# Scatters of a routing table without an order between them, and a prologue spread over two queues: a fused attention and two-layer mixture-of-experts kernel

## The chip, the cores and the metric

The kernel runs on one core of a Trainium2 chip. The core has TensorE for matrix products (PE in the rows, its weight loads PEld), VectorE (DVE), ScalarE (ACT), GpSimd (POOL), and SyncE (SP), which here only issues transfers. ScalarE and GpSimd issue transfers too; each engine works through its own list in order, so a transfer that has to wait for something holds up all that stands behind it on that engine. The metric is the device time of one execution in microseconds (us).

## The reference, cut to what matters

Three layers follow each other. First comes attention with a decay: 2 batches, 8 heads, 768 positions, 64 numbers per head, in blocks with a running state.

```python
Dmask = np.where(rel >= 0, lam[:, None, None] ** rel[None, :, :], 0.0)
lam_pow = lam[:, None, None] ** (pos[None, :, None] + 1)
...
intra = np.einsum('bhic,bhjc->bhij', qb, kb) * Dmask[None]
intra = np.einsum('bhij,bhjd->bhid', intra, vb)
inter = np.einsum('bhid,bhde->bhie', qb * lam_pow[None], kv_state)
out[:, :, sl] = intra + inter
kv_state = lam_block[None, :, None, None] * kv_state + np.einsum('bhsd,bhse->bhde', kb_dec, vb)
```

Its output, 1536 rows of 512 numbers, goes through two mixture-of-experts layers with 8 experts each. A row goes to the one expert with the largest logit, and is weighted with that expert's probability:

```python
expert_idx = np.argmax(logits, axis=1)
...
for e in range(E):
    mask = expert_idx == e
    h = np.maximum(x[mask] @ w1[e], 0.0)
    out[mask] = gate_w[mask, None] * (h @ w2[e])
```

So the rows have to be sorted by expert between the layers. The kernel does that through tables in device memory (HBM).

## The kernel before, in words

**Attention** runs over 12 tiles of 128 rows, one per stage `s` of a loop; the two batches alternate. Stage `s` computes the scores of tile `s` (`st_A`, L420), lets GpSimd scale its operands (`st_pool`: `qd` L433, `kd` L437, `ds` L444), multiplies the scores by the decay mask `Dm` on VectorE (L425), turns the finished tile `s-2` into rows and stores it to the table of rows `xd` (`st_rows`, L496 to L503), and finishes tile `s-1` (`st_B`: L456 with `qd`, L461 with the masked scores; `st_S` L475 for the state). The output needs `qd` of a tile one stage after GpSimd is to make it. `load_X` (L141) loads tile `s+3`, 1 MB, at the end of a stage, into four buffers. From stage 5 on SyncE also loads one 512 KB block of weights of the first expert per stage (`raw`, L354), and from stage 6 on ScalarE copies one block per stage (`whi`, L361) ahead of the next stage's own copies.

**Routing of the first layer** is done beside it. `st_pick` finds a row's expert, `st_rank` its place in that expert's list (`posk`), and after every three tiles `Gates` computes the probabilities into `rec1`. Then `scat` (L550) sends the three tiles' records to `tab1` in HBM: an indirect transfer per tile, issued by GpSimd, 128 records of 8 bytes, to places that `posk` gives. The program's dependency tracking sees twelve writes to one table and lets each wait until the one before has landed. They are issued in stages 5, 8 and 11, three at a time, and the last three, of the tiles `LATE`, after the loop. The first expert's list is read from the table at the end of stage 11 (`tb0`, L615), without the tiles in `LATE`, which are brought in by matrix products (L584). Rows are then gathered (L636), transposed (L655), and the first expert starts (L825). The next expert's list (`tb`, L747) is read after all twelve scatters; its rows are gathered at L768 and transposed at L788.

**The second table** `tab2` has its own sixteen scatters (L960). Those go through `put`, which declares that they don't depend on each other and lets GpSimd write one number after each (`gap`, L281); `after_puts` lets a reader of the table wait for all of them.

**The prologue** makes the powers of `lam` by eight short steps on VectorE (L191, L194), which double the number of powers each time, sends them to HBM (`F_d`, L196), and reads them back in two shapes: the decay mask `Dm` (L201, two halves of 256 KB, made of 512-byte pieces) and `qtab` (L207). All of these are in SyncE's list, between the first loads of `X`; `emb`, `tau` and `wgs` are sent from ScalarE's (L145 to L147).

A completed transfer is seen through one of eight semaphores that SyncE's and ScalarE's transfers take in turn, so the ninth transfer waits until the first has landed, and so on. The `init_dram` transfers (L225 to L232) clear the tables after stage 1.

Of the kernel before, what the change touches and what calls it, by code (L numbers as in the profile page):

```python
# [15 lines left out]
AF = mybir.ActivationFunctionType  # L16
ALU = mybir.AluOpType
# [58 lines left out]
def body(ctx, tc, nc, A, O):  # L76
# [5 lines left out]
    tab1 = dram.tile([E * TS, 2], I32, name="tab1")  # L82
# [108 lines left out]
    nc.vector.tensor_copy(out=F_s[:, 128:129], in_=lam)  # L191
    for s in range(7):
        n = 1 << s
        nc.vector.tensor_scalar(out=F_s[:, 128 + n:128 + 2 * n], in0=F_s[:, 128:128 + n],  # L194
                                scalar1=F_s[:, 127 + n:128 + n], scalar2=None, op0=ALU.mult)
    nc.sync.dma_start(out=F_d, in_=F_s)  # L196
    load_X(1, 0)
    f0 = F_d[0:8, :]
    Dm = ac.tile([128, 8, 128], F32, name="Dm")
    for g in range(2):  # L200
        nc.sync.dma_start(  # L201
            out=Dm[:, 4 * g:4 * g + 4, :],
            in_=bass.AP(tensor=f0.tensor, offset=f0.offset + 256 * g, ap=[[1, 128], [512, 4], [1, 128]]))
    load_X(1, 1)
    qtab = ac.tile([128, 4, 128], F32, name="qtab")
    for hh in range(2):
        nc.sync.dma_start(out=qtab[64 * hh:64 * hh + 64],  # L207
                          in_=bass.AP(tensor=f0.tensor, offset=f0.offset + 256 * hh + 128,
                                      ap=[[0, 64], [512, 4], [1, 128]]))
    load_X(2, 0)  # L210
    load_X(2, 1)
    load_X(3, 0)
    load_X(3, 1)
# [59 lines left out]
    puts = []  # L273
    gap = const.tile([1, 1], F32, name="gap")

    def put(inst):

        for p in puts:
            tc.declare_no_dep(inst.ins, p.ins, reason="distinct rows")
        puts.append(inst)  # L280
        nc.gpsimd.memset(gap, 0.0)  # L281

    def after_puts(inst):
        for p in puts:
            tc.add_manual_dep(inst.ins, p.ins.name, mybir.DependencyInfo(mybir.DependencyClass.Sync, mybir.DependencyReason.DATA), reason="rows of the table")
# [441 lines left out]
    class Expert:  # L727
# [601 lines left out]
```

## Time and profile before

| | us |
|---|---|
| median of 3 runs | 499.51 (494.91 to 502.37) |
| the profiled execution's own time | 493.88 |
| its span, first to last instruction | 492.1 |
| TensorE busy | 433.0 (88%) |
| VectorE busy | 336.9 (68%) |
| ScalarE busy | 269.7 (55%) |
| GpSimd busy | 226.1 (46%) |

The mean granted clock of TensorE was 0.961 of full speed. Busy shares are averages over the attention loop (about the first 94 us) and two layers of experts; they say little about the loop. The views below are read for single stretches instead. In the timeline a row is: start in us, duration in us, engine, line, operation, output and inputs, and in brackets how long the engine had been idle before and what ended that; `SPq`, `ACTq` and `POOLq` are an engine's issuing side. Several equal instructions are merged into one row with a count.

### The profile page before, as it was taken

What the parts mean: (1) busy time and instruction counts of PE and PEld (TensorE: products, weight loads), DVE (VectorE), ACT (ScalarE), POOL (GpSimd) and SP (SyncE); (2) the same over time, 40 slices, a digit from 0 to 9 for tenths busy, and PEclk for the clock granted to TensorE, in tenths of its full rate; (3) what the DMA queues carried; (4) which work ended last, traced back from release to release, by engine and by line L of the source; (5) the groups of instructions that cost most, each with busy time, mean ns of one, the idle gap of its engine ahead of it and who ended that gap; (6) DMA issues with size and microseconds to landing.
All of it is one profiled execution on the core that took longest, in us unless ns stands there. A gap on an engine that the chain in (4) does not pass through costs nothing. (4 is left out here: it accounts for less than half of the span.)

```text
span 492.1 us, 9560 instructions
## 1 busy us (share of the span) xinstructions
PE 433.0 (88%) x3482; PEld 375.2 (76%) x3484; DVE 336.9 (68%) x714; ACT 269.7 (55%) x443; POOL 226.1 (46%) x224
## 2 busy tenths in 40 slices
PE   7696577759699999999999898999999999999980
PEld 3585566549578898988888797878987788988970
DVE  5454282525569888989888966853858588989950
ACT  2244253404467575665767445645768585776830
POOL 4641725415262738375574634403435725545520
PEclk9999697978899999999999999999999999999996
DMA  6998283231958485867658246483767767786400
GB/s 199 338 345 291 96 291 75 52 125 10 356 173 281 159 283 168 286 188 264 221 190 277 85 170 206 139 259 129 260 213 247 268 206 250 245 265 244 152 25 15
DMA packets 36693, 99.00 MB, mean 201 GB/s; under 512 B 10524, under 2 KB 12068, under 8 KB 35617
## 3 DMA queue, kind: packets, MB, share of 16 engines
q1 hardware_dynamic: 31569, 88.02, 53.7%
q0 software_dynamic: 4768, 10.28, 6.7%
q8 instruction: 29, 0.48, 0.4%
q14 instruction: 23, 0.19, 0.1%
q10 hardware_dynamic: 304, 0.03, 0.0%
HBM read 87.65 MB, written 11.21 MB: 201 GB/s over the span
## 5 line engine op out<-in xcount | busy, mean ns | idle before, releaser
L379 DVE SCALAR_TENSOR_TENSOR wlo<-raw,whi 128x1024 f16<-128x1024 f32 x98 | 128.8, 1316 | 33.0 <-ACT whi L361 32.1
L361 ACT ACTIVATE whi<-raw 128x1024 fp32r<-128x1024 f32 x128 | 131.3, 1050 | 5.2 <-DMA raw<-in_wa_dram 5.2
L373 POOL TENSOR_TENSOR wlr<-raw,whi 128x1024 fp32r<-128x1024 f32 x30 | 73.7, 2457 | 112.3 <-ACT whi L361 90.1
L795 PE MATMUL pm<-xT,whi 128*128 128x416 f32 (+8 forms) x416 | 99.2, 364 | 6.7 <-DVE xT L577 3.2
L795 PE MATMUL pm<-ht,whi 128*128 128x416 f32 (+7 forms) x384 | 86.7, 362 | 0.0
L795 PEld LDWEIGHTS pm<-xT,whi 128*128 128x128 f32 x416 | 68.8, 189 | 12.4 <-DVE xT L577 5.1
L795 PEld LDWEIGHTS pm<-ht,whi 128*128 128x128 f32 x384 | 66.8, 191 | 2.0
L801 PEld LDWEIGHTS <-wlo 128*128 128x128 f16 x720 | 57.2, 98 | 14.0 <-issue 8.6
L801 PE MATMUL pm<-xH,wlo 128*128 128x208 f16 (+11 forms) x512 | 59.4, 259 | 0.6 <-DVE xH L580 0.6
L845 ACT ACTIVATE ht<-t 128x416 fp32r<-128x416 f32 (+11 forms) x64 | 35.9, 561 | 27.4 <-DVE t L839 27.1
L851 DVE SCALAR_TENSOR_TENSOR ht<-t,ht 128x416 fp32r<-128x416 f32 (+11 forms) x64 | 42.6, 666 | 7.9 <-ACT ht L845 7.9
L838 ACT ACTIVATE t<-pm 128x416 f32<-128x416 f32 (+8 forms) x52 | 26.3, 506 | 33.9 <-PE pm L795 33.7
L839 DVE SCALAR_TENSOR_TENSOR t<-pm,t 128x416 f32<-128x416 f32 (+8 forms) x52 | 29.7, 571 | 14.8 <-ACT t L838 14.1
L960 POOL DMA_INDIRECT tab<-rec,pi x16 | 27.8, 1739 | 21.1 <-issue 7.3
L550 POOL DMA_INDIRECT tab<-rec,posk x12 | 11.9, 995 | 46.9 <-DMA tab<-rec,posk 25.4
L801 PE MATMUL pm<-ht,wlr 128*128 128x208 f32 (+8 forms) x208 | 33.4, 282 | 0.0
L967 POOL DMA_INDIRECT out_y_dram<-yr,tb x17 | 19.3, 1137 | 30.0 <-ACT yr L928 21.5
L574 ACT ACTIVATE xT<-pt 128x384 fp32r<-128x384 f32 (+9 forms) x33 | 16.8, 513 | 23.8 <-PE pt L788 11.9
L801 PEld LDWEIGHTS pm<-ht,wlr 128*128 128x128 f32 x208 | 29.1, 190 | 0.4
L768 POOL DMA_INDIRECT xr<-y2d,tb x17 | 24.1, 1416 | 9.3 <-issue 7.5
L801 PE MATMUL pm<-hh,wlo 128*128 128x208 f16 (+8 forms) x208 | 26.2, 256 | 0.0
L768 POOL DMA_INDIRECT xr<-xd,tb x14 | 23.4, 1670 | 4.4 <-issue 3.1
(197 smaller groups left out, 715.5 us busy)
## 6 DMA issues: line engine op xcount, KB each, us to landing
raw<-in_wa_dram SPq DMA_DIRECT2D x64, 512.0 KB, 5.5
raw<-in_wb_dram SPq DMA_DIRECT2D x64, 512.0 KB, 4.1
X<-in_att_dram SPq DMA_DIRECT2D x8, 1024.0 KB, 7.7
X<-in_att_dram SPq DMA_DIRECT2D x8, 512.0 KB, 6.1
xd<-xr SPq DMA_DIRECT2D x12, 256.0 KB, 4.6
y2d<-yr SPq DMA_DIRECT2D x2, 416.0 KB
y2d<-yr SPq DMA_DIRECT2D x2, 384.0 KB, 3.3
Dm<-F_d SPq DMA_DIRECT2D x2, 256.0 KB
```

Of the source, the lines that this page charges most:

```text
L361: nc.scalar.activation(out=f, in_=self.raw[g], func=AF.Copy, scale=self.scale(g))
L373: (nc.gpsimd if self.pat[g] == "p" else nc.vector).tensor_tensor(out=t.rearrange("p a b -> p (a b)"), in0=self.raw[g], in1=self.hi[g].rear ...
L379: nc.vector.scalar_tensor_tensor(out=t.rearrange("p a b -> p (a b)"), in0=self.raw[g], scalar=SW, in1=self.hi[g].rearrange("p a b -> p (a ...
L768: nc.gpsimd.indirect_dma_start(out=xr[0:n], out_offset=None, in_=self.rows, in_offset=bass.IndirectOffsetOnAxis(ap=idx[:, j, 0:1], axis=0))
L795: nc.tensor.matmul(pm[:, j, 0:2 * W].rearrange("p (a w) -> p a w", a=2), wh, s2, start=first, stop=last)
L801: nc.tensor.matmul(pm[:, j, 0:self.W], wl, sh, start=False, stop=False)
L838: nc.scalar.activation(out=t1, in_=pm[:, :, W:2 * W], func=AF.Copy, scale=sc)
L839: nc.vector.scalar_tensor_tensor(out=t2, in0=pm[:, :, 0:W], scalar=sc, in1=t1, op0=ALU.mult, op1=ALU.add)
L845: nc.scalar.activation(out=ht[:, :, 0, :], in_=t2, func=AF.Relu)
L851: nc.vector.scalar_tensor_tensor(out=ht[:, :, 1, :], in0=t2, scalar=0.0, in1=ht[:, :, 0, :].bitcast(F32), op0=ALU.max, op1=ALU.subtract)
L960: i = nc.gpsimd.indirect_dma_start(out=tab2[:, :], out_offset=bass.IndirectOffsetOnAxis(ap=self.pi[:, j:j + 1], axis=0), in_=rec2[0:n, rb[ ...
L967: i = nc.gpsimd.indirect_dma_start(out=O["y"], out_offset=bass.IndirectOffsetOnAxis(ap=self.tb[:, j, 1:2], axis=0), in_=self.yr[0:n, j, :] ...
```

## The change: what it does

Three things are changed.

- `scat` goes through `put` with a list of its own, `puts1`: the scatters of `tab1` no longer depend on each other, and GpSimd writes the `gap` number after each. The readers of the table (`tb0`, `tb`) wait for all the scatters recorded so far.
- The three scatters that were issued at the end of stage 5 are issued one per stage, in stages 6, 7 and 8 behind that stage's `st_pool`; those of stage 8 in stages 9, 10 and 11. Those of stage 11 and of `LATE` stay where they were.
- `lam`'s powers are made by ScalarE; `F_d`, `Dm` and `qtab` are sent from ScalarE's queue. SyncE issues the four halves of `X` for tiles 0 and 1 first, then `emb`, `tau`, `wgs`, then tiles 2 and 3.

```diff
     load_X(0, 0)
     load_X(0, 1)
-    nc.scalar.dma_start(out=emb, in_=A["emb"])
...
+    load_X(1, 0)
+    load_X(1, 1)
+    nc.sync.dma_start(out=emb, in_=A["emb"])
+    nc.sync.dma_start(out=tau, in_=A["tau"].to_broadcast([128, 1]))
+    nc.sync.dma_start(out=wgs, in_=A["wg"])
+    for i in (2, 3):
+        load_X(i, 0)
+        load_X(i, 1)
...
-    nc.vector.tensor_copy(out=F_s[:, 128:129], in_=lam)
...
-    nc.sync.dma_start(out=F_d, in_=F_s)
+    nc.scalar.activation(out=F_s[:, 128:129], in_=lam, func=AF.Copy)
+    for k in range(7):
+        n = 1 << k
+        nc.scalar.activation(out=F_s[:, 128 + n:128 + 2 * n], in_=F_s[:, 128:128 + n], func=AF.Copy,
+                             scale=F_s[:, 127 + n:128 + n])
+    nc.scalar.dma_start(out=F_d, in_=F_s)
...
-    def put(inst):
+    def put(inst, to=puts):
 
-        for p in puts:
+        for p in to:
             tc.declare_no_dep(inst.ins, p.ins, reason="distinct rows")
-        puts.append(inst)
+        to.append(inst)
         nc.gpsimd.memset(gap, 0.0)
...
     def scat(it):
-        nc.gpsimd.indirect_dma_start(out=tab1[:, :], out_offset=bass.IndirectOffsetOnAxis(ap=posk[:, it:it + 1], axis=0),
-                                     in_=rec1[:, it, :], in_offset=None)
+        put(nc.gpsimd.indirect_dma_start(
+            out=tab1[:, :], out_offset=bass.IndirectOffsetOnAxis(ap=posk[:, it:it + 1], axis=0),
+            in_=rec1[:, it, :], in_offset=None), puts1)
...
-    gates = None
+    gates, ready = None, []
     for s in range(12):
         ps = psf[s] if s < 2 else st_A(s)
         st_pool(s)
+        if ready:
+            scat(ready.pop(0))
...
         if gates:
             gates.gate()
-            for it in range(s - 5, s - 2):
-                scat(it)
+            ready += range(s - 5, s - 2)
             gates = None
+            while s == 11 and ready:
+                scat(ready.pop(0))
```

On **GpSimd**, in the loop from stage 5 to stage 8 (`tab_62` is `tab1`, `rec_69` is `rec1`), before:

```order
L433 TENSOR_TENSOR qd<-X,qtab 128x512
L437 TENSOR_TENSOR kd<-X,Dm 128x2x4x64
L444 TENSOR_TENSOR ds<-st_183,qtab 128x256
L550 DMA tab_62<-rec_69,posk 13312x2 x3
L433 TENSOR_TENSOR qd<-X,qtab 128x512
L437 TENSOR_TENSOR kd<-X,Dm 128x2x4x64
L444 TENSOR_TENSOR ds<-st_182,qtab 128x256
L433 TENSOR_TENSOR qd<-X,qtab 128x512
```

The three scatters of stage 5 stand in one row ahead of `qd` of stage 6. On the same engine in the changed kernel, from stage 5 on:

```order
L432 TENSOR_TENSOR qd<-X,qtab 128x512
L436 TENSOR_TENSOR kd<-X,Dm 128x2x4x64
L443 TENSOR_TENSOR ds<-st_192,qtab 128x256
L432 TENSOR_TENSOR qd<-X,qtab 128x512
L436 TENSOR_TENSOR kd<-X,Dm 128x2x4x64
L443 TENSOR_TENSOR ds<-st_191,qtab 128x256
L549 DMA tab_62<-rec_69,posk 13312x2
L280 MEMSET gap 1x1
L432 TENSOR_TENSOR qd<-X,qtab 128x512
L436 TENSOR_TENSOR kd<-X,Dm 128x2x4x64
```

Each scatter now stands behind a whole stage's products, alone, with its `gap` write. On **SyncE**, at the start of the program before:

```order
L134 DMA lam<-in_lam_dram 8x1
L141 DMA X<-in_att_dram 128x1024 x2
L196 DMA F_d<-F_s 8x256
L141 DMA X<-in_att_dram 128x1024
L201 DMA Dm<-F_d 128x4x128 x2
L141 DMA X<-in_att_dram 128x1024
L207 DMA qtab<-F_d 64x4x128 x2
L141 DMA X<-in_att_dram 128x1024 x4
```

and of the change:

```order
L134 DMA lam<-in_lam_dram 8x1
L141 DMA X<-in_att_dram 128x1024 x4
L147 DMA emb<-in_emb_dram 8x512
L148 DMA tau<-in_tau_dram 128x1
L149 DMA wgs<-in_wg_dram 128x32
L141 DMA X<-in_att_dram 128x1024 x4
L141 DMA X<-in_att_dram 128x2048
```

`F_d`, `Dm` and `qtab` have left SyncE's list, and `emb`, `tau` and `wgs` have come into it behind the halves of tiles 0 and 1. They now stand in **ScalarE's** list, behind the steps that make the powers:

```order
L199 ACTIVATE F_s<-F_s 8x64
L201 DMA F_d<-F_s 8x256
L205 DMA Dm<-F_d 128x4x128 x2
L210 DMA qtab<-F_d 64x4x128 x2
L261 ACTIVATE esq,ess<-emb 8x512
```

The work on `emb` stands behind all of them on that engine.

## Rows read from the trace of the kernel before

**Rows 1.** Waits from 0 to 160 us: total us, times, longest.

```profile
POOL tab L550 <- DMA tab<-rec,posk: 25.4, 8, 6.8
```

**Rows 2.** Timeline, stages 5 to 8.

```profile
38.50 1.16 POOL L550 DMA_INDIRECT tab<-rec,posk  x1 [3.30 <-DVE m L508]
...
42.73 1.16 PE L420 MATMUL ps<-X 64*128 64x128 f32 x16
...
46.45 0.96 POOL L550 DMA_INDIRECT tab<-rec,posk  x1 [6.79 <-DMA tab<-rec,posk]
...
54.43 1.97 PE L456 MATMUL px<-qd,st 64*64 64x128 f32 x16 [9.46 <-POOL qd L433]
...
58.62 1.16 PE L420 MATMUL ps<-X 64*128 64x128 f32 x16
```

**Rows 3.** Timeline, stages 10 and 11.

```profile
70.41 1.16 PE L420 MATMUL ps<-X 64*128 64x128 f32 x16
...
77.47 1.97 PE L456 MATMUL px<-qd,st 64*64 64x128 f32 x16 [4.83 <-POOL qd L433]
...
82.08 1.16 PE L420 MATMUL ps<-X 64*128 64x128 f32 x16
```

**Rows 4.** GpSimd's groups, 0 to 95 us: busy us, mean ns, idle before.

```profile
L433 POOL TENSOR_TENSOR qd<-X,qtab 128x512 f32<-128x512 f32 x10 | 12.6, 1264 | 6.9 <-DMA X<-in_att_dram 5.5 <-PE px L456 1.4
L437 POOL TENSOR_TENSOR kd<-X,Dm 128x512 f32<-128x512 f32 x10 | 10.6, 1057 | 8.8 <-DMA Dm<-F_d 7.5 <-DMA X<-in_att_dram 1.1 <-PE pst L475 0.2
...
L444 POOL TENSOR_TENSOR ds<-st,qtab 128x256 f32<-128x256 f32 x8 | 5.9, 741 | 0.0
```

**Rows 5.** Windows: length, busy of PE, PEld, DVE, ACT, POOL, PEclk, DMA, GB/s.

```profile
37.40:42.73 5.33, 5.05 (x81) 4.30 (x80) 2.97 (x15) 2.54 (x6) 1.16 (x1) 1.00 0.90 319
56.00:58.00 2.00, 2.00 (x30) 1.67 (x29) 0.00 (x0) 0.04 (x1) 2.00 (x2) 0.66 0.00 0
```

**Rows 6.** Timeline: the first weight block, its issue and its first use.

```profile
37.61 0.87 SPq L354 DMA_DIRECT2D raw<-in_wa_dram  x1
...
45.22 1.06 ACT L361 ACTIVATE whi<-raw 128x1024 fp32r<-128x1024 f32 x1 [2.56 <-DMA raw<-in_wa_dram]
```

**Rows 7.** Timeline, end of the loop: first and third scatter, list, transposes.

```profile
87.38 1.01 POOL L550 DMA_INDIRECT tab<-rec,posk  x1 [5.93 <-DVE m L508]
...
92.21 0.97 POOL L550 DMA_INDIRECT tab<-rec,posk  x1 [1.44 <-DMA tab<-rec,posk]
...
94.34 0.34 SPq L615 DMA_DIRECT2D tb<-tab  x1
...
104.37 0.69 PE L655 MATMUL pt<-ident,xr 108*128 108x108 f32 x4 [4.16 <-DMA xr<-xd,tb]
```

**Rows 8.** Timeline: first and third scatter of LATE, second list, its transposes.

```profile
111.82 1.00 POOL L550 DMA_INDIRECT tab<-rec,posk  x1 [8.70 <-DVE cm L694]
...
117.87 0.97 POOL L550 DMA_INDIRECT tab<-rec,posk  x1 [2.32 <-DMA tab<-rec,posk]
...
120.03 0.41 SPq L747 DMA_DIRECT2D tb<-tab  x1
...
132.20 0.84 PE L788 MATMUL pt<-ident,xr 117*128 117x117 f32 x4 [4.63 <-DMA xr<-xd,tb]
```

**Rows 9.** The second table's scatters by their line: duration ns min/median/max.

```profile
L960 POOL DMA_INDIRECT tab<-rec,pi x16: 932/1959/2127, 162.1 to 306.5; - x16
```

**Rows 10.** Timeline, prologue: wgs sent and used, powers, mask, tile 2's scores.

```profile
1.82 0.44 ACTq L147 DMA_DIRECT2D wgs<-in_wg_dram  x1
...
2.34 3.12 DVE L194 TENSOR_SCALAR F_s<-F_s 8x1 f32<-8x1 f32 x7
...
7.53 0.18 DVE L221 COPY wgp<-wgs 128x32 f32<-128x32 f32 x1 [0.96 <-DMA wgs<-in_wg_dram]
...
13.29 1.89 DVE L425 TENSOR_TENSOR m<-ps,Dm 128x512 f32<-128x512 f32 x3 [1.46 <-DMA Dm<-F_d]
...
17.93 1.16 PE L420 MATMUL ps<-X 64*128 64x128 f32 x16 [2.34 <-DMA X<-in_att_dram]
```

More of the change, by code (lines that the diff above doesn't have):

```diff
@@ L189, in body @@
             nc.gpsimd.memset(wtab[:, i, (r + 7) % 8:(r + 7) % 8 + 1], float(WS[r]))
-    nc.vector.tensor_copy(out=F_s[:, 128:129], in_=lam)
[L192 to L195, printed above, removed]
-    nc.sync.dma_start(out=F_d, in_=F_s)
-    load_X(1, 0)
+    nc.scalar.activation(out=F_s[:, 128:129], in_=lam, func=AF.Copy)
[4 more added lines that the diff above has]
+    nc.scalar.dma_start(out=F_d, in_=F_s)
     f0 = F_d[0:8, :]
@@ L200, in body @@
     for g in range(2):
-        nc.sync.dma_start(
+        nc.scalar.dma_start(
             out=Dm[:, 4 * g:4 * g + 4, :],
             in_=bass.AP(tensor=f0.tensor, offset=f0.offset + 256 * g, ap=[[1, 128], [512, 4], [1, 128]]))
-    load_X(1, 1)
     qtab = ac.tile([128, 4, 128], F32, name="qtab")
     for hh in range(2):
[L207 to L213, printed above, removed]
+        nc.scalar.dma_start(out=qtab[64 * hh:64 * hh + 64],
+                            in_=bass.AP(tensor=f0.tensor, offset=f0.offset + 256 * hh + 128,
+                                        ap=[[0, 64], [512, 4], [1, 128]]))
     nc.vector.reciprocal(out=itau, in_=tau)
@@ L270, in prep_emb_b, with after_puts @@
         nc.vector.tensor_copy(out=enT[:, :, 0:8], in_=pe)
-    puts = []
+    puts, puts1 = [], []
     gap = const.tile([1, 1], F32, name="gap")
-    def put(inst):
-        for p in puts:
+    def put(inst, to=puts):
+        for p in to:
             tc.declare_no_dep(inst.ins, p.ins, reason="distinct rows")
-        puts.append(inst)
+        to.append(inst)
         nc.gpsimd.memset(gap, 0.0)
-    def after_puts(inst):
-        for p in puts:
+    def after_puts(inst, to=puts):
+        for p in to:
             tc.add_manual_dep(inst.ins, p.ins.name, mybir.DependencyInfo(mybir.DependencyClass.Sync, mybir.DependencyReason.DATA), reason="rows of the table")
@@ L614, in body @@
             tb0 = sm.tile([n0, nb0, 2], I32, tag="tb0", name="tb0", bufs=1)
-            nc.sync.dma_start(out=tb0, in_=tab1_e[0, 0:W0, :].rearrange("(j p) c -> p j c", p=n0))
+            after_puts(nc.sync.dma_start(out=tb0, in_=tab1_e[0, 0:W0, :].rearrange("(j p) c -> p j c", p=n0)), puts1)
         if 1 <= s and s + 3 < 12:
@@ L747, in load_x @@
             i = nc.sync.dma_start(out=self.tb, in_=src)
-            if self.second:
-                after_puts(i)
+            after_puts(i, puts if self.second else puts1)
             self.gate = self.tb[:, :, self.nc_ - 1:self.nc_].bitcast(F32)
```

2 lines of the change are left out of this document (removed).

## The prediction

> **What bounds the kernel now.** I read the waits first, to see which queue holds others up; then the timeline of the stretch where the longest wait sits; then the windows, to see what else was idle there; last the starts of the two expert stages that read the table.
>
> The waits put GpSimd first: its scatters waited 25.4 us for the scatter before, eight times [rows 1]. That alone costs nothing; the timeline shows who pays. A plain stage takes 5.33 us, and TensorE is busy 5.05 of them [rows 5]: the loop's pace is TensorE's. Stage 7 begins at 42.73 and stage 8 at 58.62, 15.89 us [rows 2]. In it the second scatter left at 46.45, after 6.79 us of waiting for the first one, issued at 38.50 and taking 1.16 to issue. Behind the third scatter stands `qd` of tile 6, and TensorE idled 9.46 us for it. Then the product itself took 1.97 us, and in the window at 56 the granted clock averages 0.66, between the levels of 1.2 and 2.4 GHz [rows 5]: the idle engine had lost its clock. The same again, smaller: stage 10 begins at 70.41, stage 11 at 82.08, with 4.83 us of idling before its `qd` product [rows 3]. The third and fourth chains stand where the table is read: TensorE idled 4.16 us before the first gathered rows [rows 7] and 4.63 us before the second expert's [rows 8].
>
> **The change, part by part.**
>
> *Spaced scatters in the loop.* Stages 7 and 10 exceed a plain stage by 15.89 - 5.33 = 10.56 and 11.67 - 5.33 = 6.34, together **16.9 us**, the half clock included. The new order has one scatter per stage behind that stage's `qd`, `kd` and `ds`. It waits for `rec1`, complete a stage earlier, and for no scatter. GpSimd's stage is 1.26 + 1.06 + 0.74 = 3.06 us [rows 4] plus a scatter of 1.16 [rows 2], at worst the 2.13 of the second table's, which run beside more VectorE work [rows 9]; a `gap` write lies between nothing and the 0.74 of `ds`, and for one number I take 0.3, an estimate, with the gaps around it. So 4.5 us, at most 5.9 if both bounds held, against 5.33; and `qd` is wanted one stage after it is made, which covers the excess for the six stages concerned. Spacing costs nothing as long as that stage of slack stands.
>
> *What is late next.* The stalls were also time for the transfers: in the window at 56 the DMA share is 0.00, in stage 6 it is 0.90 at 319 GB/s [rows 5]. Without the stalls a stage asks for 1 MB of `X`, 0.5 MB of weights and 0.25 MB of stored rows: 1.75 MB (1.84 million bytes) in 5.33 us is 344 GB/s, a little above those 319. And ScalarE takes its weight block in order: the block asked for at 37.61 was used at 45.22, 7.6 us later, after 2.56 us of waiting, with the copies of two tiles queued behind it [rows 6]. Stages 7 to 10 would repeat that. By the 319 a stage takes 1.84 / 0.319 = 5.8 us, 0.45 longer; over the five stages that carry both loads and blocks that is 2.2, and I take **2.5 us lost**. The ends: 0, since TensorE itself did not stop in stage 6, and 5, if the 2.56 of waiting came through twice.
>
> *Scatters of stage 11.* First to third took 92.21 - 87.38 = 4.83 us [rows 7]. Unordered, a step is a scatter of 1.01 and the 0.3 above: 2 x 1.3 = 2.6, so `tb0` is asked for **2.2 us** earlier. At the second table's 2.13 a step is 2.4 and the gain nothing; with the gap write free it is 2.8. I take the row of the same line and place. Behind `tb0` on SyncE stand a weight block and the store of tile 10's rows, both needed or waited for by the gather; they move with it. TensorE's own work was done 4.16 us before the gather landed [rows 7], so the whole 2.2 arrives.
>
> *Scatters of LATE.* 117.87 - 111.82 = 6.05 [rows 8]; 6.05 - 2.6 = **3.4 us**, ends 1.2 and 4.0. The list at 120.03 waits for the last landing; the 4.63 us of TensorE's wait for that expert's rows cover it. The sixteen weight loads behind it move forward too.
>
> *The prologue.* Two things held stage 2 until 17.93: the second half of `Dm`, first used at 13.29, and tile 2's `X`, for which TensorE idled 2.34 us [rows 10]. With all `X` issued early the second wait goes: +2.34 at best. Against it `Dm` now runs beside `X` from another queue, where in SyncE's order it stood ahead of tile 1's second half and of tile 2. The nearest row is `wgs`: 16 KB sent from ScalarE's queue at 1.82 beside the first 1 MB of `X`, and used only at 7.53, 5.7 us later [rows 10]. `Dm` has the same small pieces and thirty times the bytes. If it waits for the 1 MB of tile 1's second half and tile 2 (3.3 us at 319 GB/s) it lands at 16.6, and stage 2, which in this trace started 4.6 us after the use of the second half, 2.34 of that waiting for `X`, starts at 16.6 + 2.3 = 18.9, 1.0 later. The powers move from a 3.12 us chain on VectorE [rows 10] to ScalarE, of which the trace has no such chain: between half and twice that, 1.6 earlier to 3.1 later for `Dm`. I take the same length, since both chains are of fixed costs. VectorE's first mask also stands behind `wgp<-wgs`, and `wgs` now leaves behind tile 1; if it lands at 11 instead of 7.53 it reaches no further than `Dm` does. Between -1.0 and +2.3 I take **0**, nearer to `wgs`; with the powers the ends are +2.3 and -4.1.
>
> On the choice of engine for the powers, the Trainium skill speaks against it: in "ScalarE: Activation LUTs", Rules for kernel authors, multiplications belong on VectorE; yet the same page (What ACT_TABLE_LOAD costs) puts an activation with a pointer operand at about 280 ns, by which eight would take 2.2 us, an estimate, and the term would be +0.9. No run here shows it.
>
> *Clock.* The fourth expert-stage wait stays partly, so I count no clock gain after the loop.
>
> Sum: 16.9 + 2.2 + 3.4 + 0 - 2.5 = 20.0 us. The profiled execution took 493.88 itself, which gives 473.9. It lies 5.6 below the median of 499.51, and all three runs shown lie above it (from 494.91); the stalls are of transfers under load and vary, and those that remain will less. I forecast **475**.
>
> **The rivals.**
>
> *Everything lands.* `X` and weights keep up, tile 2's wait goes, and TensorE keeps its clock between the loop and the first expert: 16.9 + 2.6 + 3.9 + 2.3 = 25.7, and 1 to 2 for the clock: 493.9 - 27 = **467**. For it: a DMA share of 0.00 for whole windows, which is room; against it, `wgs`. In the Trainium skill, "DMA: Bandwidth & Descriptors" (Queues, rings and completion order), each DMA engine takes turns between queue rows packet by packet; by that rule `Dm` need not wait until `X` has drained, and the prologue term is the +2.3. The 5.7 us of `wgs` speak against it [rows 10]. Chance 0.2.
>
> *The transfers become the bound.* With a scatter in flight, which took 1.16 + 6.79 us to land [rows 2], a DMA share of 0.90 moved only 319 GB/s [rows 5]; if stages 6 to 10 run at 6.5 us, 5 x 1.2 = 6 are given back beyond the 2.5, and the prologue's low end takes 3: 475 + 9 = **484**. Chance 0.2.
>
> *The scatters gain nothing.* GpSimd's issue of unordered scatters takes long enough, beside VectorE, that `qd` is late again, or a wait the listing does not show stays: the 16.9 shrink to a few us, **492**. Against it: no scatter in the loop waits for another, and the second table's cost 2.13 at most [rows 9]. Chance 0.05.
>
> *Slower.* One place: ScalarE's in-order wait for its weight block. If with full queues a block lands much later than 7.6 us after its issue [rows 6], each of stages 6 to 10 is longer by the excess, TensorE waiting for ScalarE's copies of the logits and rows. It cancels the 20.0 + 2.5 at an excess of 22.5 / 5 = 4.5 us per stage, blocks landing after 12 us. At 14 us after issue, 6.5 per stage, the kernel takes 493.9 + 10 = **504**. Against it: 344 GB/s asked beside 319 seen is too little excess for that. Chance 0.03.
>
> **How the numbers follow.** The forecast has 0.52; its own range from the terms' ends is 468 to 481. The rest are the four above. The range 462 to 487 takes in the first two rivals with their spread, and leaves out the last two and some of the edges, about 0.15 to 0.2. A change of under 2% of this kernel, 10 us, could hardly be told from none, its runs differing by 1.5%: faster by more needs under 489.5, which the forecast and the first two rivals meet but for the upper edge of the second; 0.88 faster, 0.09 the same, 0.03 slower.
>
> **What would show it.** Right: no stage of the loop over 7 us; `qd` off TensorE's waits; the first `tb` request some 2 us after the third scatter of three issued 1.3 us apart; LATE's likewise. The prologue: the first use of `Dm`'s second half near 13 to 16 us and no wait for `X` at stage 2. Wrong: ScalarE's waits for `raw` of 3 us and more in each of stages 7 to 10, scatters of 2 us on GpSimd in the loop, or `Dm` landing past 18 us. What would make it wrong by most is a stall I call removed whose place another transfer takes at the same spot: TensorE idling in stage 7 for `X` instead of `qd`.

## The result and the profile after

The changed kernel takes 481.29 us (median of four, 479.79 to 482.38) against 499.11 (494.91 to 502.37): a ratio of 0.9668, interval [0.9599, 0.9737]. That is faster, and inside the range; the forecast of 475 was 6 us too low. The medians are 17.8 us apart, the profiled executions, 479.79 and 493.88, 14.1: that of before was 5.2 below its median, that of the changed kernel 1.5. What is said of stretches below holds for these two executions.

The loop first, as before in stages 5 to 11 [rows 2, 3]. The timeline of the changed kernel, start and duration in us (L419 opens a stage, L455 is the `qd` product, L549 a scatter, L360 the high half of a weight block, L506 the pick):

```profile
47.52 1.16 PE L419 MATMUL ps<-X 64*128 64x128 f32 x16
...
52.52 1.16 PE L419 MATMUL ps<-X 64*128 64x128 f32 x16
...
55.97 1.06 ACT L360 ACTIVATE whi<-raw 128x1024 fp32r<-128x1024 f32 x1 [3.52 <-DMA raw<-in_wa_dram]
...
59.32 0.39 PE L506 MATMUL bq<-gsum,lT 128*128 128x8 f32 x2 [2.05 <-DVE sh L537]
...
59.64 1.16 PE L419 MATMUL ps<-X 64*128 64x128 f32 x16
...
61.03 0.99 POOL L549 DMA_INDIRECT tab<-rec,posk  x1 [0.51 <-DVE m L507]
...
63.16 1.97 PE L455 MATMUL px<-qd,st 64*64 64x128 f32 x16
...
68.14 1.16 PE L419 MATMUL ps<-X 64*128 64x128 f32 x16
...
73.14 1.16 PE L419 MATMUL ps<-X 64*128 64x128 f32 x16
```

Stages 7 and 10 are 5.00 us each, where they were 15.89 and 11.67. The scatter at 61.03 waits for no other, and no `qd` product waits for GpSimd. But stage 9, from 59.64 to 68.14, takes 8.50, against 5.27 before: ScalarE waited 3.52 us for its weight block in stage 8, TensorE 2.05 for the gate (the short chain of steps on ScalarE and VectorE that makes three tiles' probabilities) behind that, and in stage 9 the `qd` product ran 1.97 us, as after the old stalls. The windows name it. Their columns are length, busy time of PE, PEld, DVE, ACT and POOL, granted clock, DMA share and GB/s:

```profile
36.00:40.00 4.00, 4.00 (x41) 3.00 (x39) 3.06 (x13) 1.76 (x5) 2.23 (x4) 0.63 1.00 407
60.00:64.00 4.00, 3.40 (x38) 2.57 (x36) 3.86 (x13) 2.15 (x5) 1.60 (x3) 0.62 0.77 235
64.00:68.00 4.00, 4.00 (x46) 3.56 (x42) 0.02 (x1) 1.22 (x3) 2.35 (x3) 0.53 0.96 352
```

A mean of 0.62 or 0.63 is about three quarters of a window at the lower level of 1.2 GHz, 0.53 nearly all of it. TensorE is busy for 3.40 to 4.00 us of each window, most of it at half speed.

The end of the loop and LATE, for [rows 7, 8]: scatters one and three, the list (L618, L750), the first transposes of the gathered rows (L658, L790):

```profile
78.43 0.97 POOL L549 DMA_INDIRECT tab<-rec,posk  x1 [4.42 <-DVE m L507]
...
80.98 0.97 POOL L549 DMA_INDIRECT tab<-rec,posk  x1 [0.22 <-issue]
...
83.90 0.34 SPq L618 DMA_DIRECT2D tb<-tab  x1
...
94.02 0.69 PE L658 MATMUL pt<-ident,xr 108*128 108x108 f32 x4 [3.86 <-DMA xr<-xd,tb]
...
102.06 1.01 POOL L549 DMA_INDIRECT tab<-rec,posk  x1 [9.22 <-DVE cm L697]
...
104.67 0.97 POOL L549 DMA_INDIRECT tab<-rec,posk  x1 [0.21 <-issue]
...
107.63 0.41 SPq L750 DMA_DIRECT2D tb<-tab  x1
...
119.78 0.62 PE L790 MATMUL pt<-ident,xr 117*128 117x117 f32 x4 [2.19 <-DMA xr<-xd,tb]
```

First to third is 2.55 and 2.61 us. From the third scatter to the list it is 2.92 and 2.96, where it was 2.13 and 2.16: behind an unordered three the list leaves 0.8 us later.

The prologue, for [rows 10]:

```profile
4.77 0.55 ACTq L201 DMA_DIRECT2D F_d<-F_s  x1
...
9.61 0.99 ACTq L205 DMA_DIRECT2D Dm<-F_d  x2
...
12.03 0.63 ACT L261 ACTIVATE esq<-emb 8x512 f32<-8x512 f32 x1 [7.29 <-issue]
...
14.94 0.56 PE L268 MATMUL bq<-ident,emb 8*128 8x8 f32 x4 [5.27 <-DVE emb L264]
...
16.52 2.07 POOL L436 TENSOR_TENSOR kd<-X,Dm 128x512 f32<-128x512 f32 x2 [10.57 <-DMA Dm<-F_d]
...
19.96 1.16 PE L419 MATMUL ps<-X 64*128 64x128 f32 x16
```

The powers leave at 4.77, 0.7 earlier than before, and are in HBM only at 9.61, when `Dm` is asked for. Stage 2 starts at 19.96 against 17.93, with no wait for `X`. At stage 5 TensorE waits 1.25 us for it (0.48 before).

**Four stretches.** Three count matmuls cut a run: one as the first expert starts (A, up to it), one where the second table's first expert is chosen (M, between the two), one when that expert starts (S). What is left after it is 186.4 to 186.6 us in all fourteen profiles. Starts are from the timelines; S is explained under e8. The profiled executions of e3 and e7 were over 1.5% longer than the shortest of their runs, so no stretch is read from them.

| kernel | median us | profiled | A | M | S |
|---|---|---|---|---|---|
| before | 499.11 | 493.88 | 109.27 | 165.06 | 31.34 |
| changed | 481.29 | 479.79 | 99.50 | 160.60 | 31.49 |
| e1 scatters only | 482.68 | 483.16 | 96.03 | 160.70 | 38.04 |
| e2 prologue only | 505.69 | 504.36 | 114.91 | 166.57 | 34.61 |
| e4 spaced, ordered | 491.54 | 491.42 | 101.27 | 164.74 | 37.17 |
| e5 emb early | 485.71 | 480.62 | 100.23 | 160.43 | 31.76 |
| e6 X(1) behind F_d | 483.75 | 480.72 | 100.94 | 159.41 | 32.06 |
| e8 e1 + spin at switch | 481.57 | 484.42 | 101.69 | 161.04 | 33.21 |
| e9 changed + spin in loop | 480.71 | 476.89 | 97.05 | 160.15 | 31.45 |
| e10 all three edits | 479.81 | 480.61 | 97.59 | 161.52 | 33.09 |
| e11 all three, old prologue | 477.33 | 477.88 | 94.58 | 160.76 | 34.08 |
| e12 changed again | 481.52 | 479.36 | 99.31 | 160.59 | 31.30 |

From before to changed: A -9.77, M -4.46, S +0.15, together -14.1.

Of M's 4.46, 2.65 lie between the count matmul and the first transposes (22.93 and 20.28 us: the list is asked for 2.64 earlier behind its first scatter), and 1.60 between these and a product that both kernels have (14.18 and 12.58). There TensorE waited 4.63 us before the change and ran at half clock behind it; after 2.19 us it did not. Before, then changed, product and window:

```profile
146.38 1.53 PE L795 MATMUL pm<-xT,whi 128*128 128x468 f32 x6 [0.58 <-DVE t L839]
...
132.00:136.00 4.00, 3.80 (x15) 3.51 (x16) 1.47 (x3) 0.98 (x2) 0.00 (x0) 0.57 0.95 354
```

```profile
132.36 1.53 PE L797 MATMUL pm<-xT,whi 128*128 128x468 f32 x6 [0.57 <-DVE t L841]
...
120.00:124.00 4.00, 4.00 (x30) 3.83 (x29) 2.85 (x6) 2.96 (x5) 0.00 (x0) 1.00 0.94 354
```

The twelve profiles that are read agree: this stretch takes 14.1 to 15.0 us in the four with half clock in it (before, e2, e4, e10), 12.5 to 13.5 in the eight without.

### The profile page after: what moved, and what is told of

The parts are those of the page before. It is cut to its first block, busy times and chain, and to the rows that moved or that the text cites. A ratio compares the mean times of both kernels' runs of the same rounds, so it can differ in the third digit from the quotient of the medians.

```text
span 478.0 us, 9573 instructions
## 1 busy us (share of the span) xinstructions
PE 434.2 (91%) x3482; PEld 376.0 (79%) x3484; DVE 330.0 (69%) x706; ACT 272.2 (57%) x451; POOL 226.1 (47%) x236
## 4 chain that ended last, share of the span: by engine, by line
PE 55%; DVE 16%; DMA 10%; issue 8%; ACT 6%; POOL 3%; POOLq 0%; ACTq 0%; SPq 0%; DVEq 0%
PE pm L797 19%; PE pm L803 11%; DVE wlo L378 5%; PE pm L827 4%; ACT whi L360 4%; DMA xr<-xd,tb 3%; PE px L460 2%; PE pm L904 2%; PE pm L905 2%; PE pm L906 2%; PE pt L790 2%; DMA raw<-in_wa_dram 2%; PE px L455 2%; DVE xH L580 2%; PE pb L929 1%
## 5 line engine op out<-in xcount | busy, mean ns | idle before, releaser
L360 ACT ACTIVATE whi<-raw 128x1024 fp32r<-128x1024 f32 x128 | 131.2, 1050 | 6.2 <-DMA raw<-in_wa_dram 6.1
L797 PE MATMUL pm<-ht,whi 128*128 128x416 f32 (+7 forms) x384 | 85.5, 358 | 0.0
L797 PEld LDWEIGHTS pm<-xT,whi 128*128 128x128 f32 x416 | 68.8, 189 | 12.5 <-DVE xT L577 5.1
L853 DVE SCALAR_TENSOR_TENSOR ht<-t,ht 128x416 fp32r<-128x416 f32 (+11 forms) x64 | 40.2, 629 | 7.9 <-ACT ht L847 7.9
L841 DVE SCALAR_TENSOR_TENSOR t<-pm,t 128x416 f32<-128x416 f32 (+8 forms) x52 | 29.7, 571 | 14.8 <-ACT t L840 14.1
L770 POOL DMA_INDIRECT xr<-y2d,tb x17 | 23.1, 1361 | 7.9 <-issue 7.7
L884 ACT ACTIVATE t<-pm 128x416 f32<-128x416 f32 (+7 forms) x24 | 12.1, 506 | 23.1 <-PE pm L797 21.8
```

Source lines behind the costliest of these rows:

```text
L360: nc.scalar.activation(out=f, in_=self.raw[g], func=AF.Copy, scale=self.scale(g))
L770: nc.gpsimd.indirect_dma_start(out=xr[0:n], out_offset=None, in_=self.rows, in_offset=bass.IndirectOffsetOnAxis(ap=idx[:, j, 0:1], axis=0))
L797: nc.tensor.matmul(pm[:, j, 0:2 * W].rearrange("p (a w) -> p a w", a=2), wh, s2, start=first, stop=last)
L841: nc.vector.scalar_tensor_tensor(out=t2, in0=pm[:, :, 0:W], scalar=sc, in1=t1, op0=ALU.mult, op1=ALU.add)
L853: nc.vector.scalar_tensor_tensor(out=ht[:, :, 1, :], in0=t2, scalar=0.0, in1=ht[:, :, 0, :].bitcast(F32), op0=ALU.max, op1=ALU.subtract)
```

## The experiments

The first four ran on one chip (before: median 502.63), e5 to e8 on a second occasion (499.46), e9 to e12 on a third (501.80).

**e1: the scatters without the prologue.** The changed kernel with the sends and the powers of before (lines 145 to 213 there).

```diff
-    nc.scalar.dma_start(out=F_d, in_=F_s)
+    nc.sync.dma_start(out=F_d, in_=F_s)
...
```

> The scatters as in the change, the prologue as before. Theory A: the new prologue costs the changed kernel time itself (stage 2 began at 19.96 against 17.93) and starts the half clock and the wait for X around stage 5, together 2.0 + 2.8; then stage 2 begins at 17.9 here, stages 5 and 6 take 5.1 to 5.5 each, and the span is 478.0 - 4.8 = about 473. Rival B: what is lost in stages 5 to 9 comes from the transfers and ScalarE's wait for its weight block, whatever the prologue: stage 2 at 17.9 but stages 5 to 9 as in the changed kernel, span 476.

482.68 (481.36 to 483.16), ratio 0.9669 [0.9579, 0.9759]: the change's own ratio. The expert starts 3.5 us ahead of the changed kernel's, and S takes back 6.5. Both theories were too low: neither had S in it. Nor is theory A's 2.0 of the prologue in the 3.5: stage 2 starts 1.8 ahead (18.20), but stage 3 only 0.3 and stage 9 still 0.3. The lead is made in stage 9, 5.65 us against 8.50, and not by a shorter wait:

```profile
59.05 0.39 PE L507 MATMUL bq<-gsum,lT 128*128 128x8 f32 x2 [2.05 <-DVE sh L538]
...
60.00:64.00 4.00, 3.40 (x54) 2.74 (x52) 3.61 (x13) 2.41 (x5) 1.94 (x4) 1.00 0.84 239
```

The same 2.05 us at the same place left the clock at 1.00 here.

**e2: the prologue without the scatters.** The kernel before with the other half of the change.

```diff
-    nc.sync.dma_start(out=F_d, in_=F_s)
+    nc.scalar.dma_start(out=F_d, in_=F_s)
...
```

> The prologue as in the change, the scatters as before. Theory A: slower than before by 2 to 5, span 494 to 497, with the second half of Dm first used near 16.4. Rival: the early loads of X pay back once the loop runs (fewer waits for X in stages 4 to 6), span 492 or less.

501.22 to 507.01 in three executions (a fourth of 1047.75 is left out), ratio 1.0108 [0.9917, 1.0298]; stage 2 at 19.99, 2.06 after 17.93. The new prologue gains nothing by itself; whether it loses theory A's 2 to 5 us the interval does not tell.

**e3: unordered, all three at once.** As e1, without `ready`.

```diff
-            ready += range(s - 5, s - 2)
-            gates = None
-            while s == 11 and ready:
-                scat(ready.pop(0))
+            for it in range(s - 5, s - 2):
+                scat(it)
+            gates = None
```

> The prologue as before; scatters unordered but three at once at the end of stages 5, 8 and 11. Theory A: taking the order away is what removes the stalls; three issues of 1.3 hold qd up for 3.8 us, inside the stage of slack it has; within 2 us of the run with the scatters spaced. Rival: the spacing is needed, stages 7 and 10 keep 3 us or more each, the span is 5 or more above that run.

482.16 (478.97 to 487.40), ratio 0.9646 [0.9532, 0.9760]: as e1, within an interval of some 6 us to either side. No gain of the spacing shows once the order is gone. The one trace, of the 487.40, has 7.57 and 8.12 us for stages 7 and 8, but no `qd` product waits in it.

**e4: spaced, but ordered.** `ready` as in the change; plain scatters that wait for each other as before.

```diff
-        put(nc.gpsimd.indirect_dma_start(
+        nc.gpsimd.indirect_dma_start(
...
```

> The prologue as before; scatters spaced one per stage, but each waits until the one before has landed, and those of stage 11 and of LATE go one after the other. Theory A: a scatter lands in up to 8 us beside X, a stage is 5.3, so GpSimd waits up to 3 us in a stage, which qd's stage of slack covers; the loop is as fast as with unordered ones, and only the two reads of the table lose, 1.5 and 2.6: span 4 above the run with both. Rival: the waits add up over the stages and TensorE stops for qd again, 8 or more above it.

491.54 (489.10 to 492.38), ratio 0.9846 [0.9742, 0.9949]: half of the gain. LATE in its trace, with the waits of [rows 8]:

```profile
103.82 1.01 POOL L550 DMA_INDIRECT tab<-rec,posk  x1 [9.38 <-DVE cm L697]
107.00 0.98 POOL L550 DMA_INDIRECT tab<-rec,posk  x1 [2.17 <-DMA tab<-rec,posk]
110.32 0.97 POOL L550 DMA_INDIRECT tab<-rec,posk  x1 [2.34 <-DMA tab<-rec,posk]
```

M is 4.04 longer than e1's, as before's is 4.46 longer than the changed kernel's: that is LATE. First to third in stage 11 took 4.82 us against 2.54. The rest lies in A, 5.24 longer than e1's, though no `qd` product waits and stages 7 and 10 take 5.00 each: the time is the rival's, but not TensorE's stop for `qd`, and spacing alone ends those two stalls as well. Stages 8 and 9 are 2.2 and 1.4 longer than e1's: a scatter waits 2.17 us in stage 8, TensorE 4.03 for the gate (2.05 in e1), and stage 9 runs at half clock; the remaining 1.8 come from stage 11 on.

The gate's chain has a part in this that I had not asked about. On VectorE it takes 1.03 us in stage 5 before the change and 2.93 in e1, as in e4, and TensorE waits 1.57 for it. With the three scatters gone from the end of that stage, GpSimd goes on to the next tile's `qd` and `kd` at once, and a step of the chain that meets one of them ends with it. Before, then e1:

```profile
35.95 0.16 DVE L254 TENSOR_TENSOR ga<-ss,ga 128x3 f32<-128x3 f32 x1
```

```profile
36.87 1.27 POOL L433 TENSOR_TENSOR qd<-X,qtab 128x512 f32<-128x512 f32 x1 [0.63 <-PE px L456]
...
36.99 1.17 DVE L254 TENSOR_TENSOR ga<-ss,ga 128x3 f32<-128x3 f32 x1
...
39.78 0.39 PE L507 MATMUL bq<-gsum,lT 128*128 128x8 f32 x2 [1.57 <-DVE sh L538]
```

In the fourteen profiles 25 steps that write `ga` took 0.76 us and more, all in stages 5 and 8 and beside a `qd` or `kd`, and each ended within 0.05 us of its end. None is in a kernel that issues three scatters in a row there (before, e2, e3); the changed kernel has one (0.89 us, stage 8), e12 none. No run was made to hold the two apart.

**e5: emb out of ScalarE's queue behind `Dm`.** Changed kernel; the first three transfers on ScalarE's queue, emb's three ScalarE instructions ahead of `Dm`.

```diff
-    nc.sync.dma_start(out=emb, in_=A["emb"])
+    nc.scalar.dma_start(out=emb, in_=A["emb"])
...
     nc.scalar.dma_start(out=F_d, in_=F_s)
+    nc.scalar.activation(out=esq, in_=emb, func=AF.Square, accum_out=ess)
...
```

> The changed kernel, with emb, tau and wg sent on ScalarE's queue first, as before the change, and emb's square sum and root (three ScalarE instructions) between the sending of F_d and that of Dm, not behind all four. In the changed kernel ScalarE issues nothing from 5.3 to 9.61 us (F_d in flight), then Dm and qtab to 11.98, and emb's square sum starts at 12.03; PE waits 5.27 us for emb, until 14.94. Theory A (ScalarE's order costs the 2 us of the prologue): emb is ready before 10, PE has no wait for it, the first mask starts when Dm lands, by about 12.5 to 13.5 instead of 15.71, and stage 2 at about 17.5 to 18 instead of 19.96; time about 2 us under the changed kernel's 481.3, 479. Rival B (F_d's slow landing beside X sets it: 4.84 us here against 1.97 before): Dm lands no earlier than about 15.5, stage 2 stays at 19 or later, time as the changed kernel, 480 to 482.

485.71 (480.62 to 488.93), ratio 0.9687 [0.9603, 0.9772]. The queue entries and the first mask:

```profile
4.99 0.31 ACTq L201 DMA_DIRECT2D F_d<-F_s  x1
...
9.93 0.96 ACTq L211 DMA_DIRECT2D Dm<-F_d  x2
...
18.79 0.69 DVE L425 TENSOR_TENSOR m<-ps,Dm 128x512 f32<-128x512 f32 x1 [7.93 <-DMA Dm<-F_d]
```

B, and more than it said: emb was transposed at 10.16 without a wait, yet the mask waited for `Dm` until 18.79, 8.9 us after it was asked for. With the three small entries off its queue, SyncE has sent all of tiles 2 and 3 by 11.1 us, where in the changed kernel the last half left at 16.46, and `Dm` shares with them. Stage 2 starts at 23.36, 3.4 after the changed kernel's, of which 0.7 are left at the first expert.

**e6: X(1) behind F_d.** As e5, and:

```diff
-    load_X(1, 0)
-    load_X(1, 1)
...
     nc.scalar.dma_start(out=F_d, in_=F_s)
+    load_X(1, 0, nc.scalar)
+    load_X(1, 1, nc.scalar)
```

> As e5_emb_early, and X(1)'s two loads are sent on ScalarE's queue behind F_d instead of on SyncE's queue right behind X(0), so that only X(0) is in flight when F_d is sent. Theory (F_d lands late because X(1) is in flight): F_d lands about 2 us after it is sent, as before the change (5.49 to 7.46), so Dm is sent at about 7 instead of 9.61 and lands by about 11; X(1), sent at about 5.5, lands by about 9. Stage 2 at about 16 to 16.5, the earliest of all (17.93 before, 19.96 in the changed kernel); time 3 to 4 us under the changed kernel's 481.3, about 478. Rival: Dm then queues behind X(1) on the same queue and lands as late as before, stage 2 at 18 to 20, time 480 to 482.

483.75 (480.21 to 487.45), ratio 0.9658 [0.9569, 0.9748]. It doesn't test what it was made for: SyncE put tiles 2 and 3 where tile 1 had been, so `F_d` (sent 4.99, `Dm` asked for at 9.79) again ran beside bulk loads. Stage 2 at 21.59.

**e7: the high halves a stage later.** Changed kernel:

```diff
-LO_AT = {7: (0,), 8: (1,), 9: (2,), 11: (4,)}
+LO_AT = {8: (0,), 9: (1,), 10: (2,)}
...
-        if 6 <= s < 11:
+        if 7 <= s:
             wcur.split_hi(wcur.todo.pop(0))
+    wcur.split_lo(4)
```

> The changed kernel, with the high halves of expert 0's weight blocks (ScalarE) one stage later each, in stages 7 to 11 instead of 6 to 10, and the low halves of blocks 0, 1, 2 in stages 8, 9, 10, that of block 4 behind the loop. In the changed kernel the high half at 55.97 waited 3.52 us for its raw block and held the gate chain of stage 8 behind it; PE idled 2.05 us there and ran at half clock in stage 9 (8.50 us against 5.27 before the change). Theory A (the new wait is ScalarE's in-order wait for the block): no high half waits over 0.5 us for its block before stage 11, stages 8 and 9 take 5.0 to 5.6 us each instead of 7.12 and 8.50, the tail starts 4 to 5 us earlier, time about 477. Rival B (the raw loads themselves are late, and the wait moves to whoever is next): stage 8 or a later one still loses 2 us or more, and the time stays at 480 to 482.

483.80 (477.98 to 488.04), ratio 0.9644 [0.9557, 0.9732]. In the profiled execution, the longest, no high half waited for its block any more and stage 8 took 5.32 us, but stages 6 and 9 took 9.05 and 7.99, both with half clock in them; the shorter ones have no trace. The median is no lower than the changed kernel's: against A's time.

**e8: matmuls on zeros at the switch.** e1 with one number changed:

```diff
-SPL = (1, 0)
+SPL = (12, 0)
```

> The kernel with the scatters of the change and the old prologue (482.68 us, profiled 483.16), with 12 idle matmuls of 128x512 instead of 1 at the switch from the first expert table to the second, where PE otherwise waits for the rows that are gathered for the second table's first expert. There that kernel's PE waited 2.98 us (the changed kernel's 0.34), and ran at a granted clock of 0.54 in 280 to 290 us and 0.78 in 290 to 300 (the changed kernel's 1.00 and 1.00); from the last matmul of the first table (278.41) to the first count of the second (294.77) it took 16.36 us against 9.57 in the changed kernel and 9.58 before the change. Theory A (the drop in clock comes from the wait, and costs what that kernel lost against its own start): the clock stays at 1.00 there, the switch takes 11 to 12.5 us, time about 478. Rival B (the clock falls whatever PE does in the wait, or the switch is bound by the chain on VectorE and the gather): the switch still takes over 14 us, time 481 to 484.

S in e1 was 38.04 us against the changed kernel's 31.49. In e1's timeline the first rows for the second table come after a wait of 2.98, and the windows behind it are at half clock:

```profile
281.39 1.17 PE L1093 MATMUL pt<-ident,xr 112*128 112x112 f32 x4 [2.98 <-DMA xr<-y2d,tb]
...
294.77 0.17 PE L691 MATMUL pc<-acc,ones 128*1 128x8 bf16 x1
```

```profile
280.00:290.00 10.00, 8.61 (x48) 7.79 (x49) 3.36 (x22) 4.74 (x8) 1.56 (x3) 0.54 0.45 128
290.00:300.00 10.00, 10.00 (x54) 9.19 (x54) 5.95 (x17) 2.84 (x5) 2.98 (x6) 0.78 0.21 72
```

In the changed kernel the same place is

```profile
282.36 0.67 PE L1092 MATMUL pt<-ident,xr 112*128 112x112 f32 x4 [0.34 <-DMA xr<-y2d,tb]
...
291.59 0.17 PE L690 MATMUL pc<-acc,ones 128*1 128x8 bf16 x1
```

and in e8, timeline and windows:

```profile
284.11 2.77 PE L410 MATMUL pz<-wz 128*128 128x512 bf16 x12
287.18 0.67 PE L1093 MATMUL pt<-ident,xr 112*128 112x112 f32 x4 [0.31 <-DMA xr<-y2d,tb]
...
295.94 0.17 PE L691 MATMUL pc<-acc,ones 128*1 128x8 bf16 x1
```

```profile
280.00:290.00 10.00, 9.69 (x72) 7.34 (x71) 4.07 (x11) 4.10 (x7) 3.35 (x3) 1.00 0.55 176
290.00:300.00 10.00, 9.21 (x66) 8.17 (x65) 9.59 (x31) 5.06 (x10) 3.76 (x6) 1.00 0.47 144
```

The rows were as late, TensorE spent the time on zeros, the clock stayed at 1.00 and the switch took 11.8 us from 284.11, as theory A has it: S is 33.21, 4.8 less than e1's. The time, 481.57 (479.94 to 484.42), ratio 0.9645 [0.9577, 0.9712], is not clearly below e1's: in the profiled execution stretch A was 5.7 longer, in code that the two share. Of that 4.2 lie in stages 6 (8.51 against 7.15) and 9 (8.48 against 5.65): TensorE waited for the gate as long as in e1, 1.57 and 2.05 us, but the lower clock held 6.8 us behind each, in e1 3.4 behind the first and none behind the second. Why one execution falls and another does not, the rows don't show.

Why the rows take 2 to 3 us more in some executions was not found either. Eight of the fourteen profiles have it, all four of the first occasion among them. Without zeros S is then 34.6 to 38.0 (e1, e2, e4), with them 33.1 to 34.1 (e8, e10, e11).

**e9: matmuls on zeros in the loop.** Changed kernel and

```diff
+        if s in (5, 8):
+            spin(7)
         if s >= 2:
             st_pick(s - 2)
```

> The changed kernel, with 7 idle matmuls of 128x512 (about 1.5 us) ahead of the pick in stages 5 and 8, where PE waits for the gate's shift on VectorE (2.05 us in stage 8 of the changed kernel) and the stage behind runs at half clock (stage 9: 8.50 us, granted clock 0.62 and 0.53, against 5.27 before the change). Theory A (the drop in clock comes from PE's idleness around the gate): no stretch of four us between 58 and 70 us shows less than 0.9, stage 9 takes 5.3 to 6 us, the tail starts about 3 us earlier, time 478 to 479. Rival B (the stage is as long through the late weight block, whatever the clock): stage 9 stays over 7 us, time 481 to 482.

Stage 8's end, the weight block's late half first, and the windows:

```profile
56.27 1.06 ACT L360 ACTIVATE whi<-raw 128x1024 fp32r<-128x1024 f32 x1 [3.44 <-DMA raw<-in_wa_dram]
...
57.81 1.46 PE L409 MATMUL pz<-wz 128*128 128x512 bf16 x6 [0.16 <-issue]
...
60.10 1.16 PE L419 MATMUL ps<-X 64*128 64x128 f32 x16
...
65.76 1.16 PE L419 MATMUL ps<-X 64*128 64x128 f32 x16
```

```profile
60.00:64.00 4.00, 3.39 (x50) 2.71 (x49) 3.83 (x15) 2.31 (x5) 1.71 (x3) 1.00 0.83 220
64.00:68.00 4.00, 4.00 (x68) 3.40 (x68) 2.76 (x11) 1.41 (x4) 2.37 (x3) 1.00 1.05 387
```

ScalarE waits for its block as in the changed kernel, 3.44 us; the clock is 1.00, and stage 9 takes 5.66 instead of 8.50: theory A, in the trace. One trace alone could be chance, since e1 kept its clock there without zeros; but of seven profiles with the spaced scatters and no zeros in the loop (changed, e1, e4, e5, e6, e8, e12) six have half clock in stage 9, of the three with zeros (e9 to e11) none. Stage 5 does not gain: its clock is held too, and it takes 6.72 against 6.66, as the gate's chain there takes 2.91 us instead of 1.03. In time, 480.71 (476.37 to 482.92), ratio 0.9622 [0.9555, 0.9690], it is 0.8 under e12: two of six executions are under 477, four between 480 and 483, and those have no trace. That is not clear of the noise.

**e10 and e11: e7, e8 and e9 together,** on the changed kernel and on e1.

> The changed kernel with three edits: the high halves one stage later (as e7_halves_later), the 7 idle matmuls in stages 5 and 8, and 12 instead of 1 at the switch to the second table (as e8_spin_at_switch). Theory A (what the change gave back is PE's clock, lost after each wait of 2 us or more): stages 6 to 10 at 5.0 to 5.6 us each, no half clock behind stage 4, experts' start at 94 to 97, the switch 32 to 34 us, time 474 to 477. Rival B (transfers set the length of these stages and fill up whatever is gained): stages as in the changed kernel or moved by one, time 479 to 482.

> As e10_all_three, with the prologue from before the change (powers on VectorE, sent on SyncE's queue, X(1) to X(3) behind them). Theory A (the new prologue costs about 2 us at stage 2, and the transfers that it brought forward are not what the loop waits for): 1 to 3 us under e10_all_three. Rival B (what the prologue loses the loop gives back, since X and the weights are then ahead): the same time within 1 us.

e10: 479.81 (478.71 to 485.77), ratio 0.9629 [0.9556, 0.9702], above theory A's bracket and inside rival B's: stage 5 waited 2.20 us for `X` and was followed by 0.57 in 36 to 40, a place without spare matmuls, and M has half clock in it again, 161.52. "After each wait of 2 us or more", as A has it, does not hold: after 2.05 (e1), 2.19 (changed kernel, in M) and 2.35 us (e11, in M) the clock stayed at 1.00. e11: 477.33 (476.70 to 479.33), ratio 0.9562 [0.9507, 0.9618], every execution below the lowest of e12. It is the best version here, 4.2 us below the change's median and 2.5 below e10's. That is theory A's time for the prologue, but not its place: stage 2 starts 1.45 earlier than in e10, stage 3 0.2 later; the lead is made at stage 5 (33.62 against 35.67), where e11 has no wait for `X`, and in the half clock behind it. From 22 to 90 us e11's clock does not leave 1.00.

**e12: the changed kernel once more,** without an edit.

> The changed kernel once more, on the chip of the other runs of this set, for comparison. Both theories: 480 to 484 us, as the 481.29 of its first runs; where PE waits under 1 us for the gathered rows at the switch to the second table, the stretch between the two count matmuls there takes 31 to 33 us, and where it waits about 3 us, 37 to 38.5.

481.52 (479.36 to 483.04), ratio 0.9649 [0.9594, 0.9704]; S 31.30 after a wait of 0.92.

## Why the prediction was right, and where it was not

*Loop stalls, 16.9 forecast:* 15.89 + 11.67 - 2 x 5.00 = 17.56. Right, and for the reason given: `qd` stood behind scatters that waited for each other. Either half of the edit is enough for these two stalls: e3 has no order and no spacing, e4 spacing and order, and no `qd` product waits in either. What the prediction held of the spacing, that it "costs nothing", is not so: it set `qd` and `kd` beside the gate's chain (e4).

*Stage 11, 2.2 forecast, and LATE, 3.4.* The step of 1.3 was right (1.27 and 1.30). What I didn't have is the last landing, 0.8 us later in a batch: `tb0` is asked for 5.47 us after the first scatter instead of 6.96, 1.5 earlier and not 2.2; 0.8 of it is left at the first expert (A's 9.77 less the 8.94 by which stage 11 starts earlier). LATE's list is asked for 5.57 after the first scatter instead of 8.21, 2.64 earlier where I had 3.4. M is shorter by 4.46, above my upper end of 4.0: the other 1.8 are nearly all clock, the 1.60 shown under the four stretches. e4, which has that half clock too, gives 4.04.

*What is late next, 2.5 forecast, ends 0 and 5: the step that failed.* It was 6.6: stages 4, 5, 6, 8 and 9 are longer by 0.77 + 1.57 + 0.42 + 0.60 + 3.23. The wait I named was there, ScalarE's for `raw`, 3.52 us. But I priced it by transfers alone, at the rate of a stage, and took 319 GB/s for their limit; the window at 36 moved 407. In stage 9 the cost is what TensorE's idleness led to: with the same late block and the clock held it is 2.84 us less in e9, and 2.85 less in e1. Stage 5 is at half clock as well, but its 1.57 are not the clock's alone: it takes as long with the clock held (e9, 6.72; e11, 6.68), then for the gate's chain beside `qd` and `kd`. The prediction read the half clock in stage 7 [rows 5], counted it as part of the stall, and did not ask what shorter waits would do to it, nor what GpSimd's products would run beside once the scatters were gone. Why a wait lets the clock fall in one execution and not in the next stays open.

*The prologue, 0 forecast, ends +2.3 and -4.1:* -2.03 in this pair. In part that is luck of the pair: the profile of before starts stage 3 at 21.77, the earliest of these and the only one with no half clock up to there; e1, e4, e8 and e11, with the old prologue too, start it between 22.85 and 24.07, those with the change's (changed, e2, e9, e10, e12) between 23.40 and 24.38. Against those the forecast of 0 was right at this place. What the new prologue still costs comes at stage 5, where three of the five (changed, e10, e12) wait 1.2 to 2.2 us for `X` and none with the old one more than 0.5. `X` did stop being waited for at stage 2; `F_d` took 4.84 us to land beside `X` where it had taken 1.97, and e5 has `Dm` 8.9 us on the way beside more of it. The transfers' own records say why: in the changed kernel `F_d`'s 8 KB moved from 8.65 us on, when 1.97 of the 2.10 million bytes of `X` asked for ahead of it had moved; before, from 6.48 on, behind 0.94 of 1.05 million. So the bound from `wgs` [rows 10] was the right mechanism for it. By the rule of the Trainium skill, "DMA: Bandwidth & Descriptors" (Queues, rings and completion order), `Dm` need not wait until `X` has drained; here its pieces moved from 12.23 us on, when 0.32 of the 0.52 million bytes of `X` sent at the same time, 9.61, had moved, and the +2.3 that I worked out as this rule's result did not come. The powers took 0.20 + 2.35 us on ScalarE. The Trainium skill's 280 ns for an activation with a pointer operand ("ScalarE: Activation LUTs", What ACT_TABLE_LOAD costs) gave 2.2 for eight, an estimate; the trace is near it, and VectorE's 3.12 for seven lost. The 0.7 us so gained went into `F_d`'s landing.

*Clock after the loop, 0 forecast.* It gave the 1.60 in M. S has +0.15 in this pair, but e1 shows that there was something to lose: 6.5 us at the switch to the second table, from one late gather. A half clock of 10.2 us behind the wait for the first gathered rows (3.86 us, from 95.06 on; before the change 4.16, from 105.16 on) is the same in both, and no run filled that wait.

*The rivals.* "Everything lands" fell on the prologue and the half clock. "The transfers become the bound", 484, was nearer in number, 2.7 off against 6.3: stages 6 to 10 took 6.27 on average, near the 6.5 that it needs. In kind it was not: stages 7 and 10 ran at 5.00, and the excess stands in stages 8 and 9, behind one late block. The slower rival needed blocks of 12 us and more in each stage; the waits were 3.5, 1.8 and less.

Of the signs, the `qd` waits went and the steps of 1.3 us came; "no stage over 7 us" failed (7.12 and 8.50), the list left 2.9 us behind the third scatter, not 2, and `kd` had all of `Dm` at 16.5, past the 16. One sum was wrong: the terms' ends reach down to 16.9 + 0 + 1.2 - 4.1 - 5 = 9.0, which is 485, not the 481 of the forecast's own range.

Sum, in the traces: 8.94 + 0.83 + 4.46 - 0.15 = 14.1, against 20.0.

## What to carry to other kernels

Before pricing a wait that a change leaves or makes, look at the granted clock in the windows behind waits of that length, in more than one execution: here a wait of 2.05 us for the gate cost TensorE 2.84 us more at half clock in one and nothing more in another, and 2.98 us at the switch cost 4.8 more. Where such a wait can't be removed, matmuls on zeros in it are cheap, and do nothing for the wait itself. When an engine is freed, look at what it now runs beside: the steps that met GpSimd's products took up to 2.03 us instead of 0.16. A small transfer that others depend on should leave before bulk loads, not beside them from another queue.

## What the runs showed of the hardware

- TensorE idle 2.05 us ahead of stage 9 was followed by windows at a granted clock of 0.62 and 0.53 in the changed kernel and at 1.00 in e1; idle 2.98 us at the switch (e1), by 0.54 and 0.78. Filled with 128x512 products of zeros (12 in 2.77 us), the same places stayed at 1.00 (e8, e9).
- Steps of 128x3 on VectorE, 0.16 us alone, that met a 128x512 product of GpSimd (1.06 to 1.28 us) took up to 2.03 us and ended within 0.05 us of its end (e1, e4).
- Behind three unordered scatters to one table, 1.3 us apart, the reading transfer leaves 2.5 to 3.6 us after the third is issued; behind ordered ones 2.1 to 2.2.
- 8 KB sent from another queue with 1.5 MB of loads still to move landed after 4.8 us, against 1.97 with 0.5 MB still to move ahead of it in its own queue; `Dm` took up to 8.9.
- Two executions of the same attention code differed by 5.7 us at its end (e1 and e8, which are the same up to there), 4.2 of it in two stages behind waits of the same length; the last 186.4 us agreed within 0.2 in every kernel.
